# Rounding spread out, state ahead of scores, and seven masks moved off VectorE in a fused linear-attention and feed-forward kernel

## The chip, the core and the metric

The kernel runs on one core of a Trainium2 chip. The metric is the device time of one execution in microseconds. A core has five engines with instruction queues of their own, each worked through in order: TensorE (PE, with PEld for its weight loads), VectorE (DVE), ScalarE (ACT), GpSimd (POOL) and SyncE (SP), which here issues nearly all DMA transfers. Engines wait for each other through semaphores. Matmuls write to PSUM, a small memory that ScalarE and VectorE empty into SBUF.

## What is computed

There are two parts, one after the other, all in float32:

```python
# attention: 4 batches, 8 heads, 768 steps, head size 48
f = 1 / (1 + exp(-f_logit))
for t in range(S):
    state = f[:, :, t, :, None] * state + outer(k[:, :, t], v[:, :, t])
    y[:, :, t] = q[:, :, t] @ state
x = y.transpose(0, 2, 1, 3).reshape(B * S, H * D)      # 3072 x 384

# feed-forward
h = x @ w_in                                           # 384 -> 2048
g = h * erf(softplus(h))
out = g @ w_out                                        # 2048 -> 384
```

The weights arrive as 64-bit floats and are read as pairs of 32-bit words; the kernel itself rounds them to float32.

## The kernel before

The sequence is cut into 24 chunks of 128 steps, six to a batch, and into 12 blocks of two chunks. Each chunk g passes four stages.

```python
def stage_d(g):   # decays: cumulative sums of the prepared logits by a matmul with a triangle
    nc.tensor.matmul(ps, lhsT=tri[:], rhs=lts[blk][:, j, :], ...)       # L358, to PSUM pool ps_at
    nc.scalar.activation(out=dp, in_=ps, func=AF.Exp, scale=-1.0)       # L361
    nc.scalar.activation(out=kd, in_=ps, func=AF.Exp)                   # L364
    ...                                      # decay of the whole chunk, by DMA, to Tall
    nc.vector.tensor_tensor(out=qd, in0=qn, in1=dp, op=ALU.mult)        # L371
    nc.vector.tensor_tensor(out=kd, in0=kn, in1=kd, op=ALU.mult)        # L375

def stage_t(g):   # transposes of qd and kd: two PSUM tiles of ps_at, L385
    ...
    nc.scalar.copy(out=qTs[g][:], in_=pss[0][:])                        # L391
    nc.scalar.copy(out=kTs[g][:], in_=pss[1][:])                        # L393; VectorE from chunk 9

def stage_s(g):   # scores, mask, state
    sc = ps_sc.tile([P, 2, HP, P], FP32, name="sc", tag="sc")           # pool with one buffer
    ...                                                  # 8 matmuls sc <- kT, qT       L403
    ...                                                  # chunks 0-2: 4 matmuls, totals L411
    A = work1.tile([P, 2, HP, P], FP32, name="A", tag="A")              # pool with one buffer
    nc.vector.tensor_tensor(out=A, in0=sc, in1=tri (broadcast), op=ALU.mult)   # L417
    if c == NCH - 1: return
    dS = ps_at.tile([P, HP, D], FP32, name="dS", tag="at")
    ...                                                  # 8 matmuls dS <- kd, vt       L431
    for r in range(2):
        nc.vector.tensor_tensor(out=Sn, in0=dS, in1=old, op=ALU.add)           # L444
        nc.vector.tensor_tensor(out=new, in0=Sn, in1=total, op=ALU.mult)       # L447

def stage_y(g):   # y = A v + q state, 32-column matmuls L146; then xT <- y by ScalarE   L460
    ...
```

The pool `ps_at` has two PSUM buffers, shared by ps_d, ps_t, dS and y in turn. `tri` holds ones where t >= s.

The logits of a block are readied by `prepare`: VectorE clamps them (L335), ScalarE takes exp and ln (L339, L340), for which it loads another function table.

The feed-forward part of a block is `hidden` (L513: four groups of 12 matmuls `hps`, each emptied by ScalarE, L520, and followed by exp, two tanh, two VectorE products L160, a tanh L485 and a product L487) and `project` (L641: `ops`). From block 1 on `project` uses seven half-size products and sums of operands (`sum_h` on VectorE, `sum_w` on GpSimd, L541) in place of eight.

Rounding of a weight piece takes seven steps, one on ScalarE (L285) and six on VectorE (L287, 291, 296, 300, 305, 310). There are 16 pieces, eight of w_in and then eight of w_out.

The order is written by hand. An iteration emits a sequence of matmul slots (one matmul of hps or ops each; each matmul appears as two passes in the trace), and at given slots it inserts other work:

```python
for it in range(n_blocks):
    gen, n = slots(it)          # it 0: hidden of blocks 0 and 1, 96 slots; it 1: hidden of block 2, 48; ...
    if it == 0:
        todo = [(stage_d, 3), (stage_t, 3), (stage_d, 4), (stage_s, 3), (stage_t, 4), (stage_y, 3),
                (stage_d, 5), (stage_s, 4), (stage_t, 5), (stage_y, 4)] + stages(2)[4:]
        at = [3, 9, 12, 15, 20, 23, 36, 44, 60, 74, 78, 82, 86, 92]
    else:
        todo = stages(it + 2) if it + 2 < n_blocks else []
        at = [int(3 + (n - 13) / max(1, len(todo)) * i) for i in range(len(todo))]
    if it + 3 < n_blocks:
        prepare_at = at[todo.index((stage_d, (it + 3) * CPB))] - 10
    ...
    for s, _ in enumerate(gen):
        due += 1 if it == 0 and s < 48 else 0.5
        while due >= 1:
            weights_step()      # one rounding step
            due -= 1
        ...                     # the stage whose slot it is, prepare, activation steps, sums
```

The last block's output is put together by VectorE from the products (L649) and stored by one DMA:

```python
yield from products((2, 3), (5, 7, 3, 4))
plus(o[:, 5:7, :], o[:, 4:5, :].broadcast_to((P, 2, DH)), pair(5))
plus(o[:, 1:3, :], o[:, 5:7, :], pair(3))
plus(o[:, 3, :], o[:, 5, :], place[7])
store(blk)
```

Of the kernel before, what the change touches and what calls it, by code (L numbers as in the profile page):

```python
# [40 lines left out]
FP32 = mybir.dt.float32  # L41
# [4 lines left out]
ALU = mybir.AluOpType  # L46
# [21 lines left out]
P = 128  # L68
# [3 lines left out]
def kernel(  # L72
# [10 lines left out]
    nc = tc.nc  # L83
    B, H, S, D = q.shape
# [5 lines left out]
    HP = H // 2  # L90
    DP = 64
    M = 32
    NCH = S // P
    CPB = 2
    TB = CPB * P
    n_blocks = B * S // TB
# [24 lines left out]
    def rows(r, n=D):  # L121
        return slice(DP * r, DP * r + n)

    def y_matmuls(y, A, vt, qT, Mbd):

        for kt in range(n_k):
            todo = []
            for i in range(P // M):  # L130
# [5 lines left out]
                for r in heads_in:  # L136
                    o = D if (part == 1 and r == 1) else start
                    terms.append((pair[:, o : o + M], A[:, r, a, :]))
                if Mbd is not None:
# [25 lines left out]
    main = ExitStack()  # L165
    fix = main.enter_context(tc.tile_pool(name="fix", bufs=1))
    lpool = main.enter_context(tc.tile_pool(name="lpool", bufs=2))
    work = main.enter_context(tc.tile_pool(name="work", bufs=2))
    xpool = main.enter_context(tc.tile_pool(name="xpool", bufs=3))
    epool = main.enter_context(tc.tile_pool(name="epool", bufs=2))  # L170
    work1 = main.enter_context(tc.tile_pool(name="work1", bufs=1))
    ps_sc = main.enter_context(tc.tile_pool(name="ps_sc", bufs=1, space=PSUM))
# [14 lines left out]
    DH = d_model // 2  # L187
# [125 lines left out]
    FIRST = 3  # L313
    xTs, As, qTs, kTs = {}, {}, {}, {}
# [82 lines left out]
    def stage_s(g):  # L397
        b, c = divmod(g, NCH)
        qT, kT = qTs[g], kTs.pop(g)
        sc = ps_sc.tile([P, 2, HP, P], FP32, name="sc", tag="sc")  # L400
        for a in range(HP):
            for r in range(2):
                nc.tensor.matmul(  # L403
                    sc[:, r, a, :], lhsT=kT[rows(r), a, :], rhs=qT[rows(r), a, :],
                    start=True, stop=True,
                )
        if g in totals:

            pairs = dps[g % 2][:].rearrange("t (a r) d -> t a (r d)", r=2)
            for a in range(HP):  # L410
                nc.tensor.matmul(  # L411
                    totals[g][:, a : a + 1], lhsT=pairs[:, a, :], rhs=ident[:, P - 1 : P],
                    start=True, stop=True,
                )
            nc.vector.tensor_copy(out=Tall[:, g, :], in_=totals.pop(g))
        A = work1.tile([P, 2, HP, P], FP32, name="A", tag="A")
        nc.vector.tensor_tensor(  # L417
            out=A[:].rearrange("s r a t -> s (r a) t"),
            in0=sc[:].rearrange("s r a t -> s (r a) t"),
            in1=tri[:].unsqueeze(1).broadcast_to((P, H, P)),  # L420
            op=ALU.mult,
        )
        As[g] = A
        if c == NCH - 1:
            return
        dS = ps_at.tile([P, HP, D], FP32, name="dS", tag="at")
        vt, kd = vts[g % NV], kds[g % 2]
        for a in range(HP):
            for r in range(2):
                h = 2 * a + r  # L430
                nc.tensor.matmul(  # L431
                    dS[rows(r), a, :], lhsT=kd[:, h, 0:D], rhs=vt[:, a, r, 0:D],
                    start=True, stop=True,
                )
        new, old = Mbds[g % 2], Mbds[(g + 1) % 2]
        Sn = work1.tile([P, HP, D], FP32, name="Sn", tag="Sn")
        for r in range(2):
            total = Tall[rows(r), g, :].unsqueeze(2).broadcast_to((D, HP, D))
            if c == 0:
                nc.vector.tensor_tensor(  # L440
                    out=new[rows(r), :, r, :], in0=dS[rows(r)], in1=total, op=ALU.mult
                )
                continue
            nc.vector.tensor_tensor(  # L444
                out=Sn[rows(r)], in0=dS[rows(r)], in1=old[rows(r), :, r, :], op=ALU.add
            )
            nc.vector.tensor_tensor(  # L447
                out=new[rows(r), :, r, :], in0=Sn[rows(r)], in1=total, op=ALU.mult
            )
# [106 lines left out]
    def blocks(h):  # L556
        return h[:, 0:2, 0:P], h[:, 2:4, 0:P], h[:, 0:2, P:], h[:, 2:4, P:]
# [16 lines left out]
    def sum_step():  # L574
        if to_sum and next(to_sum[0], "end") == "end":
            to_sum.popleft()
# [35 lines left out]
    def project(blk):  # L612


        ops = [ps_moe.tile([P, 2, 512], FP32, name="ops", tag="moe") for _ in range(2)]
        place = {n: ops[i][:, j, k * DH : (k + 1) * DH] for n, (i, j, k) in {
            1: (0, 0, 0), 2: (0, 1, 0), 6: (0, 1, 1), 5: (1, 0, 0), 7: (1, 0, 1), 3: (1, 1, 0), 4: (1, 1, 1),
        }.items()}
        first = [1, 2, 5, 3]

        def pair(n):
            i, j = {2: (0, 1), 5: (1, 0), 3: (1, 1)}[n]
            return ops[i][:, j, 0 : 2 * DH].rearrange("p (n c) -> p n c", n=2)

        def products(gis, ns):
            for gi in gis:
                gr = groups[blk, gi]
                while gr["sums"] is None:
                    sum_step()
                a11, a12, a21, a22 = blocks(gr["h"])  # L630
                w = w_out_sb[:, FG * gi : FG * (gi + 1), :]
                s, t = gr["sums"], w_sums(gi)
                for j in range(2):
                    w1, w2 = w[:, j, :], w[:, 2 + j, :]
# [12 lines left out]

        def plus(out, x, y):
            nc.vector.tensor_tensor(out=out, in0=x, in1=y, op=ALU.add)  # L649

        o = rows_sb
        yield from products((0, 1), (1, 2, 6))
        yield from products((0,), (5, 7, 3, 4))
        to_sum.appendleft(sum_h(groups[blk, 3]))
        yield from products((1,), (5, 7, 3, 4))
        yield from products((2, 3), (1, 2, 6))
        nc.scalar.copy(out=o[:, 3, :], in_=place[1])  # L657

        plus(o[:, 0:5:4, :], o[:, 3:4, :].broadcast_to((P, 2, DH)), pair(2))
        yield from products((2, 3), (5, 7, 3, 4))  # L660

        plus(o[:, 5:7, :], o[:, 4:5, :].broadcast_to((P, 2, DH)), pair(5))
        plus(o[:, 1:3, :], o[:, 5:7, :], pair(3))
        plus(o[:, 3, :], o[:, 5, :], place[7])
        store(blk)

    def chain(*gens):
# [38 lines left out]
    with tc.manual_schedule():  # L706
# [16 lines left out]
            out=tri[:], in_=tri[:], pattern=[[1, P]], compare_op=ALU.is_ge, fill=0.0,  # L723
            base=0, channel_multiplier=-1,
# [99 lines left out]
        due = 0.0  # L824
        for it in range(n_blocks):
            gen, n = slots(it)
            if it == 0:
                todo = [(stage_d, 3), (stage_t, 3), (stage_d, 4), (stage_s, 3), (stage_t, 4), (stage_y, 3),
                        (stage_d, 5), (stage_s, 4), (stage_t, 5), (stage_y, 4)] + stages(2)[4:]
                at = [3, 9, 12, 15, 20, 23, 36, 44, 60, 74, 78, 82, 86, 92]  # L830
            else:
                todo = stages(it + 2) if it + 2 < n_blocks else []
                at = [int(3 + (n - 13) / max(1, len(todo)) * i) for i in range(len(todo))]
            if it + 3 < n_blocks:
                prepare_at = at[todo.index((stage_d, (it + 3) * CPB))] - 10
            at, todo = deque(at), deque(todo)
            for s, _ in enumerate(gen):
                due += 1 if it == 0 and s < 48 else 0.5
                while due >= 1:
                    weights_step()  # L840
                    due -= 1
# [2 lines left out]
                if at and s == at[0]:  # L844
                    at.popleft()
                    f, g = todo.popleft()
                    f(g)
                    if f is stage_y:
                        load_to(g + LOOK)
                if it == 0 and s == 5:  # L850
                    prepare(2, 0, CPB)
                if it == 0 and s == 9:
                    load_f(6)
# [18 lines left out]
                elif it > 2:  # L872
                    if s == n_o and it < n_blocks - 1:
                        to_sum.extend(sum_h(groups[it - 1, gi]) for gi in range(NS))
                    if it == n_blocks - 1 and s % n_o == 40 and s < 2 * n_o:
                        blk = n_blocks - 2 + s // n_o
# [10 lines left out]
    def general():  # L887
# [209 lines left out]
```

## Time and profile before

| | before |
|---|---|
| time, median of 3 | 637.3 us (636.75 to 637.35) |
| span of the profiled run | 635.8 us |
| TensorE busy | 610.8 us |
| VectorE busy | 428.5 us |
| ScalarE busy | 354.2 us |
| GpSimd busy | 25.7 us |
| mask product A, VectorE, L417 | 24 x 1.22 us |
| copy of 128x1024 from PSUM, ScalarE, L520 | 44 x 1.01 us |
| select of 128x128, GpSimd, L722 | 0.29 us |

In the profile a busy share is an average over the whole span; the row of forty digits shows it slice by slice in tenths, and a slice is 15.9 us long. Waits are given as "engine line of the waiting instruction <- engine line of what released it: total us, times, longest". A wait is put down to what came last. A window line gives the busy time of each engine in a stretch, then the granted clock of TensorE, the busy share of the DMA engines and their rate. A timeline line gives start, duration, engine, line, operation and its tiles, with the idle time before it in brackets.

### The profile page before, as it was taken

The numbers are of one execution on the slowest core, as the hardware profiler recorded it, in microseconds if no ns is written. First come the engines' busy times: TensorE is split into PE (matmuls) and PEld (weight loads), VectorE is DVE, ScalarE is ACT, GpSimd is POOL, SyncE is SP. The second block draws the span as 40 slices with busy tenths as digits, with TensorE's granted clock in tenths as the row PEclk, the third lists the DMA queues.
The fourth block names the chain that finished last, engine by engine and source line by source line (L and its number), as shares of the span: only waits on it lengthen the run. The fifth ranks groups of instructions, "written<-read, shape, count | busy, mean of one in ns | idle before, by whom it ended". The sixth has DMA issues, their size and how long they took to land.

```text
span 635.8 us, 11231 instructions
## 1 busy us (share of the span) xinstructions
PE 610.8 (96%) x4727; PEld 536.7 (84%) x4727; DVE 428.5 (67%) x651; ACT 354.2 (56%) x421; POOL 25.7 (4%) x24
## 2 busy tenths in 40 slices
PE   8979899999998999999999999999999999999995
PEld 6857778788667889889889989988978989989995
DVE  4799999635899576586485584495585764756741
ACT  5354456657763675756664856666566446656200
POOL 0000000000392000000000000000000000000000
PEclk9999999999999999999999999999999999999998
DMA  9998802311211131031041041031000000000000
GB/s 198 244 278 230 258 13 51 73 26 28 51 31 32 28 75 26 14 88 26 14 89 25 14 89 25 13 76 32 19 26 1 2 26 1 10 17 1 26 26 29
DMA packets 120633, 37.02 MB, mean 58 GB/s; under 512 B 112384, under 2 KB 115456, under 8 KB 120576
## 3 DMA queue, kind: packets, MB, share of 16 engines
q1 hardware_dynamic: 118496, 35.84, 24.2%
q8 instruction: 39, 0.64, 0.4%
q10 hardware_dynamic: 2080, 0.39, 0.4%
q14 instruction: 18, 0.15, 0.1%
HBM read 31.46 MB, written 4.72 MB: 57 GB/s over the span
## 4 chain that ended last, share of the span: by engine, by line
PE 72%; DVE 15%; ACT 7%; issue 3%; DMA 2%; SPq 0%; POOL 0%; DVEq 0%; ACTq 0%; POOLq 0%
PE hps L513 30%; PE ops L641 28%; PE y L146 5%; PE sc L403 3%; PE ps_t L385 2%; PE ps_d L358 2%; ACT x L155 2%; DVE e L160 1%; DVE A L417 1%; DVE scratch L541 1%; DMA Hg<-in_moe_w_in_dram 1%; DVE w_in_sb L296 1%; DVE Hg L305 1%; PE dS L431 1%; DVE Hg L487 1%
## 5 line engine op out<-in xcount | busy, mean ns | idle before, releaser
L513 PE MATMUL hps<-xT,w_in_sb 128*128 128x256 f32 x1152 | 263.9, 384 | 1.0 <-ACT xT L460 0.6
L513 PEld LDWEIGHTS hps<-xT,w_in_sb 128*128 128x128 f32 x1152 | 216.5, 191 | 35.7 <-issue 2.6
L160 DVE SCALAR_TENSOR_TENSOR e<-x,e 128x1024 f32<-128x1024 f32 x96 | 120.0, 1250 | 23.6 <-ACT x L155 23.5
L155 ACT ACTIVATE x<-Hg,serf_bias 128x1024 f32<-128x1024 f32 x88 | 97.7, 1142 | 0.1
L641 PE MATMUL ops<-wT,Hg 128*128 128x192 f32 x352 | 86.8, 328 | 0.0
L152 ACT ACTIVATE e<-Hg 128x1024 f32<-128x1024 f32 x44 | 46.5, 1058 | 70.9 <-DVE Hg L487 70.4
L641 PE MATMUL ops<-wT,scratch 128*128 128x192 f32 x320 | 75.1, 326 | 0.8 <-DVE scratch L541 0.8
L641 PE MATMUL ops<-w_out_sb,Hg 128*128 128x192 f32 x352 | 74.3, 328 | 0.0
L487 DVE TENSOR_TENSOR Hg<-Hg,e 128x1024 f32<-128x1024 f32 x44 | 54.2, 1231 | 28.7 <-ACT e L485 28.6
L520 ACT COPY Hg<-hps 128x1024 f32<-128x1024 f32 x44 | 44.4, 1009 | 50.2 <-PE hps L513 49.8
L649 DVE TENSOR_TENSOR scratch<-scratch,ops 128x384 f32<-128x384 f32 (+1 forms) x44 | 21.1, 501 | 65.3 <-ACT scratch L657 56.2
L641 PEld LDWEIGHTS ops<-wT,Hg 128*128 128x128 f32 x352 | 61.7, 190 | 2.2 <-issue 0.2
L641 PEld LDWEIGHTS ops<-w_out_sb,Hg 128*128 128x128 f32 x352 | 60.0, 190 | 3.7 <-issue 1.2
L641 PEld LDWEIGHTS ops<-wT,scratch 128*128 128x128 f32 x320 | 55.8, 190 | 1.1 <-POOL wT L541 1.1
L485 ACT ACTIVATE e<-e 128x1024 f32<-128x1024 f32 x48 | 50.5, 1052 | 6.2 <-DVE e L160 6.2
L371 DVE TENSOR_TENSOR qd<-qn,dp 128x384 f32<-128x384 f32 x24 | 13.3, 556 | 52.9 <-ACT dp L361 52.9
L417 DVE TENSOR_TENSOR A<-sc,tri 128x1024 f32<-128x1024 f32 x24 | 29.3, 1219 | 14.8 <-PE sc L403 14.6
L641 PE MATMUL ops<-w_out_sb,scratch 128*128 128x192 f32 x160 | 39.1, 326 | 0.0
L460 ACT COPY xT<-y 128x384 f32<-128x384 f32 x24 | 11.5, 479 | 45.7 <-PE y L146 45.7
L146 PE MATMUL y<-A,vt 128*32 128x128 f32 x768 | 35.2, 277 | 1.3 <-ACT qT L391 1.2
L146 PEld LDWEIGHTS y<-A,vt 128*32 128x32 f32 x768 | 27.3, 109 | 8.2 <-issue 3.8
L403 PEld LDWEIGHTS sc<-qT,kT 48*128 48x128 f32 x384 | 24.1, 193 | 7.6 <-issue 6.3
(108 smaller groups left out, 658.8 us busy)
## 6 DMA issues: line engine op xcount, KB each, us to landing
lt<-in_f_logit_dram SPq DMA_DIRECT2D x24, 192.0 KB, 3.5
qn<-in_q_dram SPq DMA_DIRECT2D x24, 192.0 KB, 3.7
out_dram<-scratch SPq DMA_DIRECT2D x12, 384.0 KB, 3.2
kn<-in_k_dram SPq DMA_DIRECT2D x23, 192.0 KB, 3.7
vt<-in_v_dram SPq DMA_DIRECT2D x23, 192.0 KB, 2.8
w_out_sb<-in_moe_w_in_dram SPq DMA_DIRECT2D x4, 768.0 KB, 6.0
Hg<-in_moe_w_in_dram SPq DMA_DIRECT2D x4, 768.0 KB, 6.7
Hg<-in_moe_w_out_dram SPq DMA_DIRECT2D x4, 768.0 KB, 6.4
```

The source lines that it names most:

```text
L146: nc.tensor.matmul(y[M * i : M * (i + 1), kt, :], lhsT=terms[n][0], rhs=terms[n][1], start=(n == 0), stop=(n == len(terms) - 1), skip_grou ...
L152: nc.scalar.activation(out=dst[:], in_=h, func=AF.Exp)
L155: nc.scalar.activation(out=dst[:], in_=h, func=AF.Tanh, bias=serf_bias[:, i : i + 1], scale=SERF_KAB[i][0])
L160: nc.vector.scalar_tensor_tensor(out=e[:], in0=x[:], scalar=SERF_KAB[i][2], in1=e[:], op0=ALU.add, op1=ALU.mult)
L403: nc.tensor.matmul(sc[:, r, a, :], lhsT=kT[rows(r), a, :], rhs=qT[rows(r), a, :], start=True, stop=True,)
L417: nc.vector.tensor_tensor(out=A[:].rearrange("s r a t -> s (r a) t"), in0=sc[:].rearrange("s r a t -> s (r a) t"), in1=tri[:].unsqueeze(1) ...
L485: nc.scalar.activation(out=e[:], in_=e[:], func=AF.Tanh, scale=SERF_C)
L487: nc.vector.tensor_tensor(out=h, in0=h, in1=e[:], op=ALU.mult)
L513: nc.tensor.matmul(hps[:, j, :], lhsT=w_in_sb[:, kt, ft * P : (ft + 1) * P], rhs=xTs[blk][:, kt, :], start=(kt == 0), stop=(kt == n_k - 1),)
L520: nc.scalar.copy(out=gr["h"], in_=hps[:])
L641: nc.tensor.matmul(place[n], lhsT=x[:, j, :], rhs=y, start=(gi == 0 and j == 0 and n in first), stop=(gi == n_g - 1 and j == 1), skip_grou ...
L649: nc.vector.tensor_tensor(out=out, in0=x, in1=y, op=ALU.add)
```

## The change

It has five parts. The masks of chunks 3 to 9 (the fourth to the tenth) are made in two steps: ScalarE copies the scores out of PSUM and GpSimd's select then zeroes what lies below the diagonal in place, so that VectorE need not do it while it rounds weights. In every chunk the products for the state, and their VectorE work, stand ahead of the scores and the mask, so that the PSUM slot of dS is released sooner. In the first iteration the stages get other slots, the wide `prepare` of block 2 moves from slot 5 to 17, that of later blocks starts 14 instead of 10 slots ahead of its stage, and the rounding steps come at a falling rate. In the last block products 5 and 7 are finished ahead of 3 and 4, which write to another PSUM bank, so that two of the closing additions can be made early. The pool of x tiles goes from three buffers to two.

```diff
-    xpool = main.enter_context(tc.tile_pool(name="xpool", bufs=3))
+    xpool = main.enter_context(tc.tile_pool(name="xpool", bufs=2))
...
     def stage_s(g):
         qT, kT = qTs[g], kTs.pop(g)
+        if g in totals:
+            ...                              # the four totals matmuls, moved up
+        if c < NCH - 1:
+            state(g, c)                      # dS matmuls, Sn, Mbd: moved up, as a function
         sc = ps_sc.tile([P, 2, HP, P], FP32, name="sc", tag="sc")
         ...                                  # scores
-        if g in totals:
-            ...
         A = work1.tile([P, 2, HP, P], FP32, name="A", tag="A")
+        if FIRST <= g < 10:                  # FIRST = 3
+            nc.scalar.copy(out=A[:], in_=sc[:])
+            flat = A[:].rearrange("s r a t -> s (r a) t")
+            nc.gpsimd.affine_select(
+                out=flat, in_=flat, pattern=[[0, H], [1, P]], compare_op=ALU.is_ge, fill=0.0,
+                base=0, channel_multiplier=-1,
+            )
+            As[g] = A
+            return
         nc.vector.tensor_tensor(...)         # the product with tri, for the other chunks
...
+        end = blk == n_blocks - 1
+        ops.append(ps_sc.tile([P, 2, 512], FP32, name="ops", tag="sc") if end else ops[1])
...
-        yield from products((2, 3), (5, 7, 3, 4))
-        plus(o[:, 5:7, :], o[:, 4:5, :].broadcast_to((P, 2, DH)), pair(5))
+        yield from products((2, 3), (5, 7))
+        if end:
+            fives()                          # the addition to o[:, 5:7]
+            plus(o[:, 3, :], o[:, 5, :], place[7])
+        yield from products((2, 3), (3, 4))
+        if not end:
+            fives()
         plus(o[:, 1:3, :], o[:, 5:7, :], pair(3))
-        plus(o[:, 3, :], o[:, 5, :], place[7])
+        if not end:
+            plus(o[:, 3, :], o[:, 5, :], place[7])
...
-                todo = [(stage_d, 3), (stage_t, 3), (stage_d, 4), (stage_s, 3), (stage_t, 4), (stage_y, 3),
+                todo = [(stage_d, 3), (stage_t, 3), (stage_s, 3), (stage_y, 3), (stage_d, 4), (stage_t, 4),
                         (stage_d, 5), (stage_s, 4), (stage_t, 5), (stage_y, 4)] + stages(2)[4:]
-                at = [3, 9, 12, 15, 20, 23, 36, 44, 60, 74, 78, 82, 86, 92]
+                at = [3, 10, 15, 22, 28, 36, 42, 47, 56, 74, 77, 82, 87, 93]
...
-                prepare_at = at[todo.index((stage_d, (it + 3) * CPB))] - 10
+                prepare_at = at[todo.index((stage_d, (it + 3) * CPB))] - 14
...
-                due += 1 if it == 0 and s < 48 else 0.5
+                due += (1 if s < 42 else 0.6 if s < 72 else 0.3) if it == 0 else 0.42 if it == 1 else 0.6
...
-                if it == 0 and s == 5:
+                if it == 0 and s == 17:
                     prepare(2, 0, CPB)
```

More of the change, by code (lines that the diff above doesn't have):

```diff
@@ L399, in stage_s @@
         qT, kT = qTs[g], kTs.pop(g)
[L400 to L406, printed above, removed]
         if g in totals:
@@ L415, in stage_s @@
             nc.vector.tensor_copy(out=Tall[:, g, :], in_=totals.pop(g))
-        A = work1.tile([P, 2, HP, P], FP32, name="A", tag="A")
+        if c < NCH - 1:
+            state(g, c)
+        sc = ps_sc.tile([P, 2, HP, P], FP32, name="sc", tag="sc")
+        for a in range(HP):
+            for r in range(2):
+                nc.tensor.matmul(
+                    sc[:, r, a, :], lhsT=kT[rows(r), a, :], rhs=qT[rows(r), a, :],
+                    start=True, stop=True,
+                )
+        A = work1.tile([P, 2, HP, P], FP32, name="A", tag="A")
+        if FIRST <= g < 10:
[4 more added lines that the diff above has]
+                base=0, channel_multiplier=-1,
+            )
+            As[g] = A
+            return
         nc.vector.tensor_tensor(
@@ L423, in stage_s, with state @@
         As[g] = A
-        if c == NCH - 1:
-            return
+    def state(g, c):
         dS = ps_at.tile([P, HP, D], FP32, name="dS", tag="at")
@@ L615, in project @@
         ops = [ps_moe.tile([P, 2, 512], FP32, name="ops", tag="moe") for _ in range(2)]
+        end = blk == n_blocks - 1
+        ops.append(ps_sc.tile([P, 2, 512], FP32, name="ops", tag="sc") if end else ops[1])
         place = {n: ops[i][:, j, k * DH : (k + 1) * DH] for n, (i, j, k) in {
-            1: (0, 0, 0), 2: (0, 1, 0), 6: (0, 1, 1), 5: (1, 0, 0), 7: (1, 0, 1), 3: (1, 1, 0), 4: (1, 1, 1),
+            1: (0, 0, 0), 2: (0, 1, 0), 6: (0, 1, 1), 5: (1, 0, 0), 7: (1, 0, 1), 3: (2, 1, 0), 4: (2, 1, 1),
         }.items()}
@@ L621, in pair @@
         def pair(n):
-            i, j = {2: (0, 1), 5: (1, 0), 3: (1, 1)}[n]
+            i, j = {2: (0, 1), 5: (1, 0), 3: (2, 1)}[n]
             return ops[i][:, j, 0 : 2 * DH].rearrange("p (n c) -> p n c", n=2)
@@ L659, in project, with fives @@
         plus(o[:, 0:5:4, :], o[:, 3:4, :].broadcast_to((P, 2, DH)), pair(2))
-        yield from products((2, 3), (5, 7, 3, 4))
-        plus(o[:, 5:7, :], o[:, 4:5, :].broadcast_to((P, 2, DH)), pair(5))
+        def fives():
+            plus(o[:, 5:7, :], o[:, 4:5, :].broadcast_to((P, 2, DH)), pair(5))
+        yield from products((2, 3), (5, 7))
[5 more added lines that the diff above has]
+            fives()
         plus(o[:, 1:3, :], o[:, 5:7, :], pair(3))
-        plus(o[:, 3, :], o[:, 5, :], place[7])
+        if not end:
+            plus(o[:, 3, :], o[:, 5, :], place[7])
         store(blk)
```

## The prediction

> **What bounds the kernel now.** I read the page's first two parts, then the matmul engine's own waits, then the span cut into 20 us windows, and last the timeline of the stretches where something was odd.
>
> ```profile
> span 635.8 us, 11231 instructions
> PE 610.8 (96%) x4727; PEld 536.7 (84%) x4727; DVE 428.5 (67%) x651; ACT 354.2 (56%) x421; POOL 25.7 (4%) x24
> ...
> PE   8979899999998999999999999999999999999995
> ...
> DVE  4799999635899576586485584495585764756741
> ```
>
> TensorE is busy for 96% of the span, so nearly all that any reordering can win is the other 25 us. The digits show where they lie: in the first fourteen slices (about 220 us) and in the last one. In slices 2 to 7 the VectorE row stands at 9.
>
> ```profile
> 40.00:60.00 20.00, 16.44 (x141) 12.62 (x140) 19.35 (x30) 11.33 (x17) 0.00 (x0) 0.91 0.93 257
> 60.00:80.00 20.00, 18.01 (x108) 15.16 (x107) 19.32 (x29) 8.88 (x10) 0.00 (x0) 0.97 0.85 250
> ...
> 220.00:240.00 20.00, 20.00 (x145) 17.41 (x145) 15.52 (x25) 11.96 (x13) 0.00 (x0) 1.00 0.32 71
> ```
>
> The columns are PE, PEld, DVE, ACT and POOL busy, the granted clock, DMA share and GB/s. From 40 to 80 us VectorE is busy 19.3 of each 20 us: it is the bound there, with the seven-step rounding of raw weights (one piece costs it 0.58+0.59+1.0+0.6+1.0+0.9, that is 4.65 us from the first step of one piece at 53.87 to the next at 58.51). From 220 us on TensorE is full, and nothing but its own work counts. The engine's waits name the holes:
>
> ```profile
> PE ps_t L385 <- DVE Sn L444: 5.9, 4, 2.1
> PE ps_d L358 <- ACT qT L391: 2.0, 1, 2.0
> ...
> PE ps_d L358 <- ACT lt L340: 1.5, 1, 1.5
> ...
> PE y L146 <- ACT qT L391: 1.2, 1, 1.2
> ```
>
> The timeline puts the four Sn waits at 77.7 (1.99 us), 168.9 (0.76), 202.6 (2.09) and 471.7 (1.07): the second transposes need a PSUM slot that holds dS, and VectorE reads dS only after the mask product A. The other three are at 43.5, 91.2 and 115.3 us.
>
> To size the pool of losses I took steady rates from the full stretch (42 hps passes in 9.26 us, 0.2205 us each; 336 ops passes in 54.61 us, 0.1625 each) and priced the passes between 32 and 215 us with them: 384 hps 84.7, ops of L596 21.2, 109 ops of L641 17.7, and about 41 for attention, together some 165 of 183 us. So about **18 us** are lost there, 13 as visible holes, the rest as pipeline refill after each hole and as two spells of half clock.
>
> **What the Trainium skill says.** "SBUF — State Buffer", section "SBUF: two separate sides": VectorE and GpSimd share a port pair that is an exclusive lock; a VectorE operation with two SBUF inputs or in a two-port mode and a GpSimd operation that reads SBUF do not overlap. The trace agrees closely. In the timeline of VectorE the same 128x256 subtraction is
>
> ```profile
> 189.70 1.22 DVE L541 TENSOR_TENSOR scratch<-Hg 128x256 f32<-128x256 f32 x1
> ...
> 195.24 0.41 DVE L541 TENSOR_TENSOR scratch<-Hg 128x256 f32<-128x256 f32 x1
> ```
>
> 1.22 us while GpSimd works through w_out sums, 0.41 us once it has stopped. "GPSIMD Engine Reference", section "3.1 Elementwise — side-by-side cycle accounting", calls GpSimd about twice as slow per element as VectorE for two-input operations; here its 128x384 sums take 1.0 us at the least, against 0.55 us for VectorE's qd product of that size. "TensorE: Matmul & The Clock Gate", section "What's actually happening", says an idle window of about 3.4 us halves the clock. Here the clock column falls to 0.50 at 45 to 48 us and 79 to 82 us, after holes of only about 2 to 4 us in pieces; two spells of 3.41 us at half rate, 1.7 us each.
>
> **The change, part by part.**
>
> (1) Masks of chunks 3 to 9 (counted from 0). VectorE loses 7 products of 1.22 us, 8.5 us. ScalarE gains 7 copies of 128x1024 from PSUM; its copy of that size (hps to Hg) takes 1.01 us, so 7.1 us, into windows where it is 40 to 75% busy. GpSimd gains 7 selects of 128x1024. The only selects before are 128x128 at 0.29 us, and a one-column memset takes 0.10 us: 0.19/127 is 1.5 ns a column, so about 1.6 us for 1024 (estimate). Where VectorE is full the lock hands this time back: each select blocks it for up to 1.6 us and saves 1.22. Up to the state update of chunk 4, two chunks: minus 2.4, plus up to 3.2 us. I book **0 us** for this part in the full stretch, and nothing elsewhere, as TensorE does not wait for A there. The longer way to A (copy 1.0, select 1.6, some 0.3 of handing over: 2.9 us) must fit between scores and y. For chunk 3 there are 7 hidden products, 14 passes, 3.1 us: just enough. For later chunks there are at least 11 slots or a transposition too, 5 us or more.
>
> (2) State products ahead of scores. Sn and Mbd move ahead of A on VectorE, or A is gone: dS is released 1.2 us sooner (the length of A). At 168.9 the hole of 0.76 with its refill closes (about 1.0); at 202.6 2.09 becomes about 0.8 (1.3 won); at 471.7, where A stays on VectorE but now comes second, 1.07 closes. In the prologue the totals fill TensorE's gap at 11.2 us (0.4 to 0.7 won), but y of chunk 2 waits for A, which now ends after four state operations of together 1.47 us instead of before them: about 0.7 lost. Prologue: 0. **Sum 3.4 us.**
>
> (3) New slots and slower rounding in the first iteration. In slots, rounding steps issued by slot 48 are 42 + 6 x 0.6 = 46 instead of 48, by slot 96 67 instead of 72; so "later" is five or so steps of 0.6 to 1.0 us, not a large shift. What matters is program order on VectorE. I listed its operations up to the end of chunk 4's state update in both programs: they are the same set, less two masks. Before, that point comes at 78.06 us with VectorE never idle for long; so it comes at about 76 to 78 us again. TensorE gets over the hole at 43.5, since the wide prepare of block 2 (ScalarE idle 4.74 us for it) moves from slot 5 to 17, and is by my count (hidden passes at 0.2205 us, attention stages at the durations of the trace) some 5 us ahead at y of chunk 3. It gives this back. VectorE ends weight piece 2 at 40.75 us as before; then come piece 3 (4.65), four steps of piece 4 (2.77), the state of chunk 3 (1.45) and two more steps (1.9), so it reaches the logits at about 51.5 us, and with ScalarE's 2 x 0.84 d of chunk 4 runs at 53.5 to 54.5, where TensorE arrives at 52.4. Piece 5 and most of piece 6 (4.65 + 3.8) follow: qd of chunk 4 at about 61 to 62, TensorE there at 58.7. The transposes of chunk 5 wait for the state at 76 to 78, TensorE there at 74.6. After that there are 18 hidden products to y of chunk 4 instead of 14, 1.8 us more. Result at y of chunk 4: 85 to 88 us, against 86.04 before. **0 us.**
> Then prepare of block 3 comes 14 slots ahead of its d instead of 10 and the slots are 77 instead of 78: VectorE reaches it at about 85 to 86 us, ScalarE is done by 88, TensorE arrives at 88 to 89. The hole at 91.2 (1.47, 1.87 on the weight load) closes: **1.7 us**. In iteration 1 the same earlier prepare saves one table load of 1.28 us and a wait of 0.84 in front of the qT copy but a mask copy of 1.0 is added: of the hole at 115.3 (1.2, 1.6 with refill) **1.0 us** is won.
>
> (4) Last block: products 5 and 7 ahead of 3 and 4, so only one of the three final VectorE additions (1.41 us together, from 628.96) stays after the last matmul. **0.9 us.** The third bank only makes this possible.
>
> (5) xpool with two buffers: both x of a group are read before the next group's first x is written in issue order. I book 0.
>
> Sum: 3.4 + 0 + 1.7 + 1.0 + 0.9 = **7.0 us**, so 637.3 - 7.0 = **630.3 us**.
>
> **Rivals.** *VectorE is really freed.* If the select does not hold VectorE up, or falls into its gaps, the full stretch shortens by up to 2.4 us, and with shorter holes one or both half-clock spells vanish (1.7 us each): another 4 to 6 us, about 625. For it: the slots look tuned by someone with a trace. Against it: 0.41 against 1.22 us above. *GpSimd and the lock cost more than the mask.* A select of 2.3 us (eight times 0.29) makes A of chunk 3 late and VectorE later by 2 us in the full stretch; with a third half-clock spell most of the gain goes: 635 to 637. For it: TensorE is to wait three times for about 2 to 3 us between 52 and 77 us in my count. *ScalarE becomes the bound.* Seven copies in its in-order queue delay qT, kT and the activations; 140 to 180 us already has it at 15.6 of 20. Against it: it waited 70 us in total for finished Hg products, so it has slack: at most 1 to 2 us.
>
> **Range and chances.** Everything won comes from a pool of about 20 us (18, the hole at 471 and the tail); to pass 2%, 12.7 us, nearly two thirds of it would have to go, which needs the first rival in full. Slower by 2% would need new losses as large as all the old ones. I take 624.5 to 635.5 for eight in ten, a little room on either side of the two rivals.
>
> **What would show it.** Right: no wait of ps_t for Sn at 168 and 472; TensorE full without holes from about 210 us on; VectorE still 19 of 20 us between 40 and 75; A's selects with VectorE operations beside them drawn out from 0.6 to 1.0 to over 1.5 us; one addition after the last matmul. Wrong: VectorE well below 18 of 20 between 40 and 80 with no holes on TensorE there (first rival), or new waits of y for a select, or of ps_t for qd above 3 us (second).

## The result, and the profile after

The changed kernel takes **630.3 us** (median; 628.3 to 632.1) where the kernel before, run beside it on the same chip, takes 637.3 us (636.8 to 638.1). The ratio is 0.989, with a 95% interval of 0.985 to 0.992: some 7 us, about 1%, inside the band of "within 2%". The sum of the prediction came out almost to the digit. The parts of it did not all do so, and the experiments are mostly about those.

From the page of the kernel after, the span, the engines' busy time, and three rows of the span in 40 slices:

```profile
span 627.5 us, 11250 instructions
PE 605.7 (97%) x4727; PEld 536.9 (86%) x4727; DVE 424.1 (68%) x644; ACT 358.3 (57%) x426; POOL 35.1 (6%) x31
...
PE   8895999899999999999999999999999999999996
...
DVE  4898996655789576667566674684594764756751
...
PEclk9997999999999999999999999999999999999999
```

The losses of TensorE, which were spread over slices 3 to 13, are now gathered in one: slice 4 (47 to 63 us) fell to 5, and its clock to 0.7. After it the row is 9 but for slice 8 and the last. VectorE did not become free: its row is still 9 in slices 3, 5 and 6. The windows of the kernel after (columns PE, PEld, DVE, ACT, POOL busy, clock, DMA share, GB/s) say the same:

```profile
40.00:60.00 20.00, 13.56 (x124) 10.34 (x123) 18.33 (x26) 6.78 (x9) 1.30 (x1) 0.83 1.06 291
60.00:80.00 20.00, 19.04 (x120) 16.30 (x119) 19.23 (x30) 14.88 (x20) 1.29 (x1) 1.00 0.62 185
80.00:100.00 20.00, 20.00 (x202) 16.77 (x201) 17.91 (x24) 11.46 (x16) 1.68 (x1) 1.00 0.29 60
```

TensorE does less between 40 and 60 us than before (13.6 against 16.4 of 20 us), and then has no hole from 80 to 100 us, where it had 1.5 us. Its waits by what ended them (total us, times, longest):

```profile
PE hps L525 <- ACT xT L472: 6.4, 1, 6.4
PE y L146 <- ACT qT L391: 2.7, 1, 2.7
...
PE ps_t L385 <- DVE Sn L456: 1.9, 2, 1.0
```

The waits for Sn fell from 5.9 us in four to 1.9 in two; those for the prepared logits (`lt`) are gone from this list; a new one of 6.4 us for a copy of xT stands at the head.

To see where the time went I took the start of the y matmuls of each chunk in both traces as milestones (chunks counted from 0) and set the time after against that before:

| stretch | change, us | expected in the prediction |
|---|---|---|
| start to y of chunk 4 (prologue, full stretch) | -1.25 | 0 |
| to y of chunk 5 (hole at 91) | -1.31 | -1.7 |
| to y of chunk 6 (hole at 115) | **+1.04** | -1.0 |
| to y of chunk 8 | -0.23 | 0 |
| to y of chunk 9 (hole at 168.9) | -0.94 | -1.0 |
| to y of chunk 10 (hole at 202.6) | -1.71 | -1.3 |
| to y of chunk 20 (steady stretch) | **-1.59** | 0 |
| to y of chunk 21 (hole at 471.7) | -1.41 | -1.1 |
| to the end (tail) | -0.90 | -0.9 |
| sum, two profiled runs | -8.3 | -7.0 |

Up to y of chunk 2 the changed kernel and its eight variants below hold the same instructions, and there this start still wanders from 29.4 to 30.2 us, so rows of some tenths are not read any further. The table compares one profiled run of each kernel: that of the changed kernel took 629.2 us, 1.1 less than the median, which is why its sum is 8.3 and not 7.0. The two bold rows differ from the prediction in sign or in kind, and very nearly cancel in its total.

**The long wait.** The timeline of TensorE has it at 54.78 us. The timeline of ScalarE after shows why (start, length, line, then in brackets the idle time before and what ended it):

```profile
51.85 0.84 ACT L339 ACTIVATE lt<-lt 128x768 f32<-128x768 f32 x1 [7.42 <-DVE lt L335]
52.73 0.84 ACT L340 ACTIVATE lt<-lt 128x768 f32<-128x768 f32 x1
53.48 0.88 ACT L285 ACTIVATE w_in_sb<-Hg 128x768 f32<-128x768 f32 x1
54.27 0.47 ACT L472 COPY xT<-y 128x384 f32<-128x384 f32 x1
```

ScalarE stood still for 7.42 us with its queue blocked by the exp of the wide prepare of block 2, whose clamp VectorE reached only behind its rounding, at 51.27 us (in the last stretch before it VectorE itself stood still for 1.05 us, at 47.2, for the DMA that brings the decay of chunk 3). The copy that TensorE needs takes 0.47 us and depends on none of that; it stood behind it in the queue. Slot 17 puts the wide prepare just ahead of this copy.

**The lock.** The timeline of GpSimd and of VectorE after, a select and the rounding step beside it, and the same rounding step without a select:

```profile
43.67 1.30 POOL L423 TENSOR_SCALAR_AFFINE_SELECT A<-A 128x1024 f32<-128x1024 f32 x1 [41.77 <-ACT A L421]
...
44.05 1.33 DVE L291 TENSOR_SCALAR w_in_sb<-w_in_sb 128x768 uint32<-128x768 uint32 x1
...
52.32 0.56 DVE L291 TENSOR_SCALAR w_in_sb<-w_in_sb 128x768 uint32<-128x768 uint32 x1
```

The step takes 1.33 us instead of 0.56. Here the moved mask spared VectorE a product of 1.22 us and took 0.77 of it back. Beside all seven selects VectorE's operations are drawn out by 4.3 us together, for 8.5 us of products spared, and its busy time fell by 4.4 us (428.5 to 424.1): about half is handed back.

### The profile page after: what moved, and what is told of

It reads as the page before. It is cut to its first block, busy times and chain, and to the rows that moved or that the text cites. A ratio compares the mean times of both kernels' runs of the same rounds, so it can differ in the third digit from the quotient of the medians.

```text
span 627.5 us, 11250 instructions
## 1 busy us (share of the span) xinstructions
PE 605.7 (97%) x4727; PEld 536.9 (86%) x4727; DVE 424.1 (68%) x644; ACT 358.3 (57%) x426; POOL 35.1 (6%) x31
## 4 chain that ended last, share of the span: by engine, by line
PE 88%; DVE 4%; ACT 3%; DMA 1%; SPq 1%; issue 1%; POOL 0%; DVEq 0%; POOLq 0%
PE hps L525 39%; PE ops L655 31%; PE y L146 6%; PE sc L414 3%; PE ps_t L385 3%; PE ps_d L358 2%; PE ops L608 1%; PE dS L443 1%; DVE scratch L553 1%; DMA Tall<-dp 1%; PE busy L348 1%; DVE e L160 1%; DMA lt<-in_f_logit_dram 1%; PE ps_d L348 1%; SPq L367 1%
## 5 line engine op out<-in xcount | busy, mean ns | idle before, releaser
L663 DVE TENSOR_TENSOR scratch<-scratch,ops 128x384 f32<-128x384 f32 (+1 forms) x44 | 21.3, 502 | 53.2 <-ACT scratch L671 44.3
L146 PE MATMUL y<-qT,Mbd 128*32 128x128 f32 x480 | 30.1, 273 | 0.0
L655 PEld LDWEIGHTS ops<-w_out_sb,scratch 128*128 128x128 f32 x160 | 27.9, 191 | 0.0
```

The source lines that it names most:

```text
L146: nc.tensor.matmul(y[M * i : M * (i + 1), kt, :], lhsT=terms[n][0], rhs=terms[n][1], start=(n == 0), stop=(n == len(terms) - 1), skip_grou ...
L655: nc.tensor.matmul(place[n], lhsT=x[:, j, :], rhs=y, start=(gi == 0 and j == 0 and n in first), stop=(gi == n_g - 1 and j == 1), skip_grou ...
```

## Experiments

Each gives the median of its runs and the ratio to the kernel before on the same chip, with its 95% interval. My theory of the result: the reordering of the state gives its 3 to 4 us whatever else is done; the masks give nothing; the early prepares empty ScalarE's queue in the steady stretch; and the first iteration is bound by VectorE's program order, so that moving the wide prepare only moves the wait. The main rival: VectorE was really relieved by the masks, and the hole at 54.78 costs what it shows.

### Masks back on VectorE

The kernel after, with all masks as the product with tri:

```diff
-        if FIRST <= g < 10:
+        if False:
```

> The changed kernel with all 24 masks on VectorE again; everything else of the change stays. Theory of the prediction: the port lock gives the mask's time back where VectorE is full, so moving the masks is worth about nothing there: 629 to 632 us, VectorE reaches the end of chunk 4's state within 1 us of the 76.7 us of the changed kernel. It may even gain a little at y of chunk 6, where the mask copy stands in ScalarE's queue ahead of qT (2.68 us wait in the changed kernel). Rival, VectorE is really freed by the move: 2.4 us later at chunk 4's state and three or more us slower in all, 633 to 637 us.

Measured: 629.1 us (628.0 to 630.6), ratio 0.987 (0.986 to 0.989); the changed kernel had 0.989 (0.985 to 0.992). The masks of chunks 3 to 9 are worth nothing that can be seen here. From the timeline of TensorE in this kernel:

```profile
50.37 0.65 PE L146 MATMUL y<-A,vt 128*32 128x128 f32 x8 [5.09 <-DVE A L429]
...
112.70 1.11 PE L146 MATMUL y<-A,vt 128*32 128x128 f32 x32 [1.69 <-ACT qT L391]
```

The hole of the full stretch is still there, only under another name: y of chunk 3 waits 5.09 us for the mask, which now stands behind rounding and behind the state's update. That update does not only queue, as the timeline of VectorE shows; it waits for the DMA of chunk 3's decay:

```profile
47.95 0.35 DVE L459 TENSOR_TENSOR Mbd<-Sn,Tall 48x192 f32<-48x192 f32 x1 [2.24 <-DMA Tall<-dp]
```

The state of chunk 4 ends on VectorE at 76.5 us, against 76.7 in the changed kernel. And the wait at y of chunk 6 is 1.69 instead of 2.68 us: the mask copy of 0.99 us on ScalarE had stood in front of qT.

### The state ahead of the scores, alone

The kernel before, with the totals and the state moved up and nothing else:

```diff
+        if c < NCH - 1:
+            state(g, c)
         sc = ps_sc.tile(...)
         ...
-        if c == NCH - 1:
-            return
-        dS = ...
```

> The kernel before, with the state products and their VectorE work ahead of scores and mask in every chunk, and nothing else. Theory of the prediction: the waits of the transposes for Sn at 168.9, 202.6 and 471.7 us close or shrink, 3.4 us, and the prologue is even: 633 to 635 us. The hole at 77.7 us shrinks by at most 1.2 us. Rival, the order inside a chunk matters only together with the masks moved: 636 to 637.5 us, the waits for Sn stay.

Measured: 633.4 us (632.8 to 635.2), ratio 0.995 (0.993 to 0.996): 3.4 us by the ratio, 4.1 by the medians, against 3.4 in the prediction. The waits of TensorE for Sn in this kernel:

```profile
PE ps_t L385 <- DVE Sn L446: 3.5, 2, 2.6
```

The holes at 168.9 and 471.7 are gone and that at 202.6 is 0.96 (at 199); by the milestones this wins 0.95, 1.13 and 1.24 us, 3.3 together. What is left, 2.58 us at 75.4, lies where VectorE is full: the state comes a product earlier in its queue, but TensorE comes earlier too. What is won up to y of chunk 4, 2.4 us, is half given back at the hole for `lt`, 2.70 us where it was 1.47. From y of chunk 10 to that of chunk 20 this kernel gains nothing: the 1.6 us of the steady stretch are not the state's.

### The masks, alone

The kernel before, with the masks of chunks 3 to 9 moved to ScalarE and GpSimd (the added branch of the change, with the state still after A).

> The kernel before, with the masks of chunks 3 to 9 made by ScalarE's copy and GpSimd's select, and nothing else. Theory of the prediction: no gain in the full stretch; where VectorE has gaps the state of chunks 8 and 9 comes 1.2 us sooner, which closes the wait for Sn at 168.9 and half of that at 202.6, about 2 us: 634.5 to 637 us. Rival, VectorE is really freed: the hole at 77.7 us closes as well and with it one spell of half clock, 631 to 634 us.

Measured: 638.6 us (636.5 to 641.8), ratio 1.002 (1.000 to 1.003): a little slower, where I had expected a small gain. In the profiled run one step of that expectation fails: the hole at 202 us, which I took to shrink as the mask left VectorE's queue, grew:

```profile
201.60 0.63 PE L385 MATMUL ps_t<-ident,kd 128*128 128x128 f32 x4 [2.87 <-DVE Sn L452]
```

It went from 2.09 to 2.87 us, and the wait for the w_out sums just ahead of it (190.4) from 0.82 to 1.32. The hole at 168.9 did close, and that at 470.7 stayed at 1.07, where the mask is on VectorE. Why the late hole grew is open. Nor does this trace show why the median is slower: it is of the fastest of 14 runs (636.5 us), and its span is 1.0 us shorter than that of the kernel before. The two parts together, 3.4 us won by one and about 1 lost by the other, leave, if they simply add, some 4 to 5 of the 7 us for slots, prepares, rate and tail.

### The wide prepare later

The kernel after, with the wide prepare of block 2 moved past the copy of xT:

```diff
-                if it == 0 and s == 17:
+                if it == 0 and s == 23:
                     prepare(2, 0, CPB)
```

> The changed kernel with the wide preparation of block 2 at slot 23 instead of 17, that is behind the copy of y of chunk 3 in ScalarE's queue. In the changed kernel hps at 54.8 us waited 6.44 us for that copy, which stood behind the preparation. Theory, VectorE's rounding is the bound up to chunk 4's state: the wait disappears at 54.8 but comes back at d or the transposes of chunk 4 and at the transposes of chunk 5, and y of chunk 4 moves by less than 1.5 us: 628.5 to 631 us. Rival, the wait itself and the half clock after it (two windows, 3.4 us) are on the path: y of chunk 4 comes 4 us or more sooner, 622 to 626 us.

Measured: 632.0 us (629.4 to 632.1), ratio 0.991 (0.989 to 0.992). The wait for xT is gone, and from the timeline of TensorE:

```profile
57.62 1.65 PE L358 MATMUL ps_d<-lt,tri 128*128 128x384 f32 x2 [7.15 <-ACT lt L340]
```

TensorE gets past the xT products and stops at the next thing that needs VectorE's clamp, for 7.15 us. The time is the same within the runs, 1.0 us above the range I had given. The rival, by which the hole at 54.78 would be won, falls. (The half clock of this run began inside the hole, at about 54.3 us, not after it.)

### The shorter prepare lead

The kernel after, with the lead of the later prepares as before:

```diff
-                prepare_at = at[todo.index((stage_d, (it + 3) * CPB))] - 14
+                prepare_at = at[todo.index((stage_d, (it + 3) * CPB))] - 10
```

> The changed kernel with the lead of prepare back at 10 slots for all later blocks; the rest stays. Theory: the earlier lead closed the hole of 1.5 us at d of chunk 6, and in the steady stretch it took the table load and exp and ln out of ScalarE's way ahead of the copy that frees a PSUM slot for hps (0.35 to 0.47 us an iteration, 1.6 us from chunk 11 to 20), but it cost about 1.0 us at y of chunk 6. So this runs 1.5 to 3 us slower than the changed kernel, 631.5 to 633.5 us, with no drift against the kernel before between chunks 11 and 20, and y of chunk 6 waits 1.5 us for qT instead of 2.7. Rival, the drift comes from the order of products 5, 7, 3, 4 or from the x pool: the drift stays, 630 to 631.5 us.

Measured: 632.4 us (631.1 to 633.0), ratio 0.992 (0.990 to 0.993). In its timeline of TensorE the hole that the prediction wanted closed is back:

```profile
90.17 0.91 PE L358 MATMUL ps_d<-lt,tri 128*128 128x384 f32 x2 [1.21 <-ACT lt L340]
```

The wait at y of chunk 6 is 1.57 instead of 2.68 us, and from chunk 10 to chunk 20 the milestones no longer drift against the kernel before (-2.76 us at both ends). So the lead of 14 has a part in all three: the gain at 91, the loss at chunk 6, and the 1.6 us of the steady stretch. In that stretch the waits that go with the short lead are 0.2 to 0.4 us at a time. They show in the queue of the weight loads alone; from 210 to 450 us of this kernel:

```profile
PEld hps L525 <- DVE scratch L663: 1.0, 3, 0.4
...
PEld ps_d L358 <- ACT lt L340: 0.3, 2, 0.2
```

The changed kernel has neither line there, the kernel before has both. At the first of them, at 261.15 us, the timeline of ScalarE has a table load, exp, ln and a second table load (254.9 to 259.2 us) ahead of the copy L671; that copy, and with it VectorE's sum L663 that frees the PSUM slot, comes late.

### Clamp early, exp and ln late

The kernel after, with the wide prepare cut in two, so that ScalarE has nothing to wait for:

```diff
-                if it == 0 and s == 17:
-                    prepare(2, 0, CPB)
+                if it == 0 and s == 10:
+                    prepare(2, 0, CPB, clamp_only=True)     # VectorE's clamp
+                if it == 0 and s == 22:
+                    prepare(2, 0, CPB, clamp=False)         # exp and ln
```

> The changed kernel, but the preparation of block 2 cut in two: VectorE's clamp at slot 10, ScalarE's exp and ln at slot 22, right behind the copy of y of chunk 3, so that ScalarE's queue waits for nothing there. Theory, VectorE's rounding is the bound up to chunk 4's state: the wait of 6.4 us at 54.8 disappears and so do the two windows of half clock, but TensorE then waits at weight pieces or at the transposes of chunks 4 and 5; y of chunk 4 at 82 to 84.5 us against 84.8, in all 628 to 630.5 us. Rival, ScalarE's queue was the bound and its wait is worth its length: y of chunk 4 at 76 to 79 us, 621 to 625 us.

Measured: 630.6 us (628.5 to 630.9), ratio 0.990 (0.988 to 0.991). No wait for xT, none for lt, and in the timeline of TensorE:

```profile
61.10 1.11 PE L388 MATMUL ps_t<-ident,qd 128*128 128x128 f32 x4 [6.54 <-DVE qd L374]
```

The third name for one hole: 6.44 for xT, 7.15 for lt, 6.54 for qd, each at the first thing that needs VectorE's next turn. What VectorE has to do before qd of chunk 4 is the same in all three. It is not busy throughout: in the three kernels it stands still for 1.05, 0.68 and 2.15 us for the DMA of chunk 3's decay, ahead of the state's update. What an earlier landing of it would be worth, no run tested. The half clock, which I had expected to go with the wait, stayed (57.0 to 64.0 us).

### The rounding slowed earlier

The last kernel with, in addition, fewer rounding steps ahead of chunk 4's operands:

```diff
-                due += (1 if s < 42 else 0.6 if s < 72 else 0.3) if it == 0 else 0.42 if it == 1 else 0.6
+                due += (1 if s < 25 else 0.5) if it == 0 else 0.5
```

> The same, and the rounding steps given out differently: one a slot up to slot 25, then one in two slots up to the end of iteration 1, so that 57 - 49 = 8 or so steps of about 0.77 us leave VectorE's queue ahead of chunk 4's state (6 us). Theory, VectorE's rounding is the bound: now chunk 4's state ends at about 70 us, TensorE does not wait for it, y of chunk 4 at 77 to 80 us, in all 622 to 626 us. Rival, something else (DMA of the raw weights, ScalarE) holds this stretch: y of chunk 4 stays above 82 us, 628 us or more.

Measured: 627.9 us (626.6 to 629.0), ratio 0.985 (0.983 to 0.986). The first of these edits that pays, and the first that changes what stands before qd in VectorE's queue:

```profile
58.21 1.12 PE L388 MATMUL ps_t<-ident,qd 128*128 128x128 f32 x4 [3.60 <-DVE qd L374]
```

I had expected y of chunk 4 at 77 to 80 us, and it came at 81.8 (84.8 in the changed kernel): the direction held, but VectorE still comes 3.6 us late, behind rounding and 0.76 us of waiting for the same DMA. The half clock stayed, a further spell came at 111.9 us, and the time is above the 622 to 626 us that I had expected.

### Every prepare split, masks on VectorE or on GpSimd

The last kernel, with the clamp of each later block six slots ahead of its exp and ln, once with all masks on VectorE and once with those of chunks 3 to 9 on ScalarE and GpSimd:

```diff
+                if it + 3 < n_blocks and s == prepare_at - 6:
+                    prepare(it + 3, 0, CPB, clamp_only=True)
                 if it + 3 < n_blocks and s == prepare_at:
-                    prepare(it + 3, 0, CPB)
+                    prepare(it + 3, 0, CPB, clamp=False)
```

> The same as the run before, with the clamp of every later prepare also 6 slots ahead of its exp and ln, and all masks on VectorE. Theory: as masks on VectorE were 1.2 us faster than on GpSimd in the changed kernel, mostly at y of chunk 6 and later, and VectorE now is not full, this is 0 to 2 us faster than the run before: 621 to 625.5 us. Rival, with VectorE no longer full the lock costs nothing and the moved masks pay: 1 to 3 us slower than the run before.

> The run before (split preparations, other rounding rate) with the masks of chunks 3 to 9 on ScalarE and GpSimd again; nothing else differs. It parts the two edits between the last two runs. Theory: the earlier clamp of later blocks closed the 2.7 us wait for qT at y of chunk 6 and is most of the 4.3 us between them; the masks are worth about 0 to 1.5 us in favour of VectorE: 623.5 to 625.5 us. Rival, the mask copies in ScalarE's queue made that wait: it comes back with 1.5 us or more, 626 to 628 us.

Measured: 623.6 us (623.3 to 625.4), ratio 0.979 (0.978 to 0.981), with the masks on VectorE; 624.5 us (620.5 to 624.8), ratio 0.979 (0.977 to 0.981), with them moved. Against the last kernel (627.9 us) the second has nothing but the split of the later prepares: 3.4 us. In it the mask copy is on ScalarE again, and still no wait at y of chunk 6 is left: it was the clamp. In the timeline of ScalarE, first kernel:

```profile
100.26 0.84 ACT L342 ACTIVATE lt<-lt 128x768 f32<-128x768 f32 x1
```

No wait ahead of the exp, where the changed kernel has 2.65 us. The holes of the two kernels differ in place: 4.59 us for the mask of chunk 3 in the first, with 1.73 us of VectorE waiting for the DMA of the decay in it, and 3.06 for qd in the second, whose profiled run is its fastest.

### One mask moved, and no rounding where TensorE waits

The first of these two, with only chunk 3's mask moved and the rounding halted for eleven slots:

```diff
-        if False:
+        if g == FIRST:
...
-                due += (1 if s < 25 else 0.5) if it == 0 else 0.5
+                due += (1 if s < 25 else 0 if s < 36 else 0.55) if it == 0 else 0.5
```

> Only chunk 3's mask on ScalarE and GpSimd, where A waited 4.6 us behind rounding on VectorE in the run with all masks there; and no rounding steps at all from slot 25 to 36, where qd of chunk 4 waited for VectorE (3.6 us), 0.55 a slot afterwards. Theory, VectorE's queue ahead of what TensorE waits for is the only loss left between 40 and 80 us: y of chunk 4 comes at 77 to 80 us against 81.4, in all 620 to 623 us. Rival, the weights then come too late and TensorE waits for pieces 6 and 7 instead: 623 to 626 us.

Measured: **619.8 us** (619.4 to 620.5), ratio 0.973 (0.971 to 0.974): under both kernels, 2.7% below the kernel before. One window of it, and its largest hole in that stretch:

```profile
40.00:60.00 20.00, 18.14 (x155) 14.32 (x154) 17.80 (x27) 9.59 (x13) 1.17 (x1) 1.00 1.05 292
```
```profile
56.14 0.66 PE L388 MATMUL ps_t<-ident,qd 128*128 128x128 f32 x4 [1.52 <-DVE qd L374]
```

18.1 us of TensorE where the changed kernel has 13.6, at full clock throughout, and y of chunk 4 at 77.0 instead of 84.8 us. The two edits were not run apart. Against the kernel with seven masks moved the gain is 4.7 us by the medians, but 1.1 by the fastest runs of each (620.5 and 619.4): a large part of it is that the runs no longer scatter.

## Why the prediction was right, and where it was not

**(1) Masks, 0 us: right in size, and for about half of the reason given.** The masks back on VectorE gave the same time, and a select drew a VectorE step out from 0.56 to 1.33 us. But the prediction had up to 3.2 us handed back for 2.4 spared in the full stretch, and the two selects there handed back 1.5. VectorE was relieved by some 0.9 us, and TensorE gained nothing from it. The tile view of A in the kernel after has the durations (ns, min/median/max):

```profile
L421 ACT COPY A<-sc x7: 988/1012/1013, 42.6 to 163.8; 128x1024 f32<-128x1024 f32 x7
L423 POOL TENSOR_SCALAR_AFFINE_SELECT A<-A x7: 1091/1299/1675, 43.7 to 164.8; 128x1024 f32<-128x1024 f32 x7
```

The copy was priced at 1.0; the select's estimate of 1.6 was too high, the median is 1.30. The drawn-out step has one input. The lock, by the Trainium skill ("SBUF — State Buffer", section "SBUF: two separate sides"), holds for VectorE operations with two SBUF inputs and for those in a two-port mode; the 0.77 us fit it, but no run shows by which of the two this step falls under it. One of the seven moves looks of use: chunk 3's mask, behind rounding and a state update that waits for a DMA, makes y wait 5.09 and 4.59 us in the two kernels that have it on VectorE. But no run moves it alone, and with all seven moved or none the medians are the same (624.5 and 623.6). The late masks have a smaller use: where they are on VectorE again the wait for the w_out sums is back with 0.6 to 0.7 us, and the stretch to y of chunk 10 gives 1.3 us instead of 1.7.

**(2) State first, 3.4 us: right in sum.** Alone it gave 3.4 to 4.1. By holes: 0.94 measured for 1.0 at 168.9; 1.71 for 1.3 at 202.6, where the state alone gave 1.24 and the wait for the w_out sums just ahead, which I had not counted, fell from 0.82 to 0.23 us; 1.41 for 1.07 at 471.7, where the state alone gave 1.13 and the short lead 1.14, so that some 0.3 us is the longer lead's. In the prologue y of chunk 2 waits 0.99 us for A; I had 0.7.

**(3) The first iteration, 0 us to y of chunk 4.** Measured -1.25, of which -0.94 after y of chunk 2. VectorE's side was right, though I had not seen its wait for a DMA (and its row stands at 9 in slices 3 to 7, not 2 to 7): I had it at the logits at 51.5 us, at qd of chunk 4 at 61 to 62 and at the end of that chunk's state at 76 to 78, and the trace has 51.27, 60.24 and 76.70. What failed is the step from there to TensorE. I gave it three waits, at d (1 to 2 us), qd (about 3) and the transposes of chunk 5 (about 2); it had one of 6.44 us for a copy of xT, and 0.96 at the last. I had followed VectorE's queue and TensorE's, and not ScalarE's, in which that copy stood behind an exp that waited for VectorE. The total was hardly touched, as whatever TensorE misses there it waits for anyway: three placings of the prepare differ by less than their runs do. The 91 us hole gave 1.31 for 1.7, and it is back in the kernel with the short lead: right.

**The failing step is y of chunk 6: 1.0 us to be won, 1.0 lost.** The table load of 1.28 us was saved as planned. But "a wait of 0.84 in front of the qT copy" was not: the exp now waits 2.65 us for the clamp of block 4, since VectorE's program order again has it late, and the mask copy adds 0.99. The timeline of ScalarE after:

```profile
106.44 0.84 ACT L339 ACTIVATE lt<-lt 128x768 f32<-128x768 f32 x1 [2.65 <-DVE lt L335]
...
110.52 0.99 ACT L421 COPY A<-sc 128x1024 f32<-128x1024 f32 x1
...
113.11 0.58 ACT L391 COPY qT<-ps_t 128x512 f32<-128x512 f32 x1
```

Masks back took one part of it away (1.69 us left), the earlier clamp all of it.

**What I left out: the steady stretch, 1.6 us won.** I had written that from 220 us on only TensorE's own work counts. Its waits of 0.2 to 0.4 us, one or two an iteration, leave the matmul queue at 10.00 of 10 us busy and show in the weight loads alone; the longer lead removes them, and without it they return. So the total is as near as it is partly since 2.0 us too few at chunk 6 stand against 1.6 and 1.25 us that I had not booked at all. That much of the agreement is luck.

**(4) Tail, 0.9: right.** Of VectorE's final additions only one, 0.56 us, comes after the last matmul; they were three with 1.41. **(5) xpool, 0:** no run isolates it, and nothing in the trace points to it. It stays open.

**Rivals.** VectorE was not freed in the changed kernel (18.3 and 19.2 of 20 us), and no half-clock spell vanished. But the rival's premise, that shorter holes take the spells with them, is in line with the last kernel: with 1.5 us as its longest hole there, no spell is left before the tail, and the kernel passes 2%. ScalarE did become a bound in one place, not by its load (6.8 of 20 us between 40 and 60) but by its order.

## What to carry to other kernels

When one engine's queue is full, moving the wait of another changes the name of the hole and not its size (6.44, 7.15, 6.54 us here): what shortened it was less work ahead of what is waited for. A wait inside the full queue, here 0.7 to 2.2 us for a small DMA, is easily missed; what it costs was not tested. Preparations that pass through two engines are best issued in two pieces, so that the second engine never stands at the head of its own queue for the first; here that was worth 3.4 us for the later blocks, though nothing for block 2, where VectorE was the bound. And work moved to GpSimd was only in part off VectorE: the lock took back about half, and moving all seven brought nothing that the medians show.

## What the runs showed of the hardware

The half-clock spells followed holes of no fixed length. The wait for qT at y of chunk 6 lasted 2.67 to 2.69 us in four kernels: in the one with the slower rounding a spell follows, from 111.9 to 115.3 us, and in the changed kernel and the two others the clock stays whole. The kernel before had a spell after 1.99 us; with the masks on GpSimd a hole of 3.06 us left the clock whole in the profiled run (mean clock 0.998, 620.5 us), while three more runs of the same kernel had 0.993 and took 624.5 to 624.8. Before the tail every spell of the twelve traces lasts about 3.4, 6.8 or 10.2 us, and where a trace has two, the second starts 34.1 (three traces) or 54.6 us after the first, 10 and 16 times 3.41. Both agree with windows of 3.41 us that run freely against the program; then it matters how a hole falls into them. The Trainium skill ("TensorE: Matmul & The Clock Gate", section "What's actually happening") speaks of an idle window of about 3.4 us; the holes of 1.99 and 2.67 us are shorter than that, and how idle a window must be is not shown. The scatter fits too: 3.9 us between the fastest and slowest run of the changed kernel, with its 6.4 us hole, and 1.1 us in the last one. No run tested it directly.
